# Row pitch of the chunk inputs, in place of a planner that reckons with the arrival of TensorE's instructions

## The chip, the cores and the metric

The kernel runs on one core of one Trainium2 chip. The metric is the device time of one execution in microseconds, lower is better. All data are float32, save the weights, whose inputs can be float64 and are then passed as pairs of 32-bit words.

## The reference

Two layers in a row. The first is a linear attention with a decay for each channel (4 batches, 8 heads, 768 steps, head size 48); the second is a feed-forward layer with a hard-swish gate on the 3072 x 384 result.

```python
for t in range(S):                                   # S = 768
    cur = einsum('bhd,bhe->bhde', u * k[t], v[t])
    y[t] = einsum('bhd,bhde->bhe', r[t], state + cur)
    state = w[t][..., None] * state + einsum('bhd,bhe->bhde', k[t], v[t])
x = y.transpose(0, 2, 1, 3).reshape(3072, 384)       # (batch*step, head*dim)
h = x @ w_in                                         # 384 -> 2048
out = (h * clip(h + 3, 0, 6) / 6) @ w_out            # 2048 -> 384
```

## The kernel before

**Attention.** The 768 steps of each batch are cut into 6 chunks of 128 steps, 24 chunks in all; the two batches of a pair take turns. A chunk's `r`, `k` and `w` come in one row for each channel: the host lays out a tensor `feat` with 112 rows for a chunk (two groups of 48 channels in 64 and 48 partitions), and one row holds 512 numbers of `r`, 512 of `k`, 520 of `w` and one number at the end that makes 1545. `load_feat` moves a chunk's rows in one DMA (chunk 0 in two: `w` first). VectorE then scans the decays backwards (`back_scan`, L509) and forwards (`fore_scan`, L518), which gives scaled copies of the keys (`K`, L529) and queries (`R`, L533, over the scan `W`). TensorE makes scores within half chunks (L584), key transposes (L600), key-value products (L686), the read of the state (L664) and of the values (L673). ScalarE writes the diagonal matrices `A` (L574), VectorE copies the masked scores over them (L591). The state between chunks is decayed and added to on VectorE or GpSimd (L613, L621, L629). For chunks 0 to 8 the product of `r` and `k` is on VectorE (L542) and its sum on TensorE (L556).

**Weights.** Sixteen fetches of 768 KB (`fetch`, L477) bring pairs of weight blocks; ScalarE and VectorE convert them in three steps (`low`, L487; `whole`, L491; `full`, L496, called join below).

**Feed-forward.** Blocks of 4 chunks (512 rows). Block 0 uses plain products (`up`, L802; `down`, L821). Blocks 1 to 5 use a scheme with fewer products and more sums (up products L916, 20 in each half; down products L971, 7 for each pair of chunks), with the clip on ScalarE (L937) and gates and sums on VectorE (L933, L941, L956, L864 to L868).

**Checks of the inputs.** Inputs are loaded once more later on (`refetch`, L1006 and L1011) and reduced on VectorE (`vet`); the result chooses at the end whether a second, general path runs. With these inputs it doesn't.

**What sets the order.** All of these are steps of a `Plan`. Each step has an engine, a duration, the steps that it follows, a key (a due time) and the buffers that it takes and when they come free. `Plan.order` goes through the steps with a clock of its own: at each turn it takes the earliest engine that can start something and, on that engine, the open step with the smallest key. The instructions are emitted in that order, and each engine runs its own in order. So a different plan gives a different order on every engine, and a wait of one instruction holds all behind it on its engine. A table `SHIFT` moves the keys of single steps by hundreds of units.

**Filler.** Until the first up product (`up0.0.0`) the planner fills the time in which it reckons TensorE idle with products of the identity by itself (`spin`, L1357; one unit has 128 columns).

**The model of instruction arrival.** TensorE's instructions come to it by DMA in portions of 256. The planner before counts the instructions of each step (`size`) and reckons in `passed` when a portion is asked for, when it is there, and how late TensorE gets; the lateness is added to the end of the step:

```python
PORTION, ASKED, NEEDED = 256, 168, 194
FETCH, BEHIND, MOST = 3.5, 1.2, 8.0
```

Portion n is asked for when TensorE passes instruction 256n+168, and instruction 256n+194 waits for portion n-1. A portion is reckoned to take 3.5 us, and up to 8 more where the data queue is behind.

Of the kernel before, what the change touches and what calls it, by code (L numbers as in the profile page):

```python
# [19 lines left out]
L = 128  # L20
HL = L // 2
# [28 lines left out]
    "feat0": -505.0, "tok0": -422.0, "own0": 1325.0, "decb0": 271.0, "feat1": -407.0, "tok1": -297.0, "feat2":  # L50
    -455.0, "above2": -94.0, "turn2": 43.0, "read2": 318.0, "R3": 518.0, "least3": 704.0, "diag03": 971.0, "turn3":
    133.0, "read3": 604.0, "fore4": 1319.0, "turn4": 269.0, "fore6": 322.0, "own6": -290.0, "mid6": 481.0, "leave8":
    47.0, "leave9": 373.0, "kvs10": -355.0, "fore11": 329.0, "diag111": 355.0, "turn11": 357.0, "mid11": 685.0,
    "fore13": -285.0, "ownu13": -163.0, "diag013": -196.0, "kvs13": -305.0, "state14": 1259.0, "read14": 59.0,
    "fore15": 1004.0, "sum15": -58.0, "diag015": -247.0, "turn15": 387.0, "kvs15": -268.0, "back16": -161.0,
    "fore16": -243.0, "diag116": 159.0, "kvs16": -365.0, "mid16": -259.0, "read16": -541.0, "diag017": -338.0,
    "kvs17": -427.0, "read17": -508.0, "feat19": 180.0, "tok19": 46.0, "fore19": 666.0, "ownu19": -1100.0, "kvs19":
    -296.0, "leave19": 261.0, "turn20": -251.0, "kvs20": -479.0, "fore21": 290.0, "mid21": -1348.0, "own22": -210.0,
    "tok23": 226.0, "diag023": -1053.0, "turn23": 79.0, "kvs23": -274.0, "read23": -1360.0, "fetch0": -479.0,
    "fetch1": -261.0, "fetch2": -344.0, "fetch3": 259.0, "fetch4": -306.0, "fetch5": 303.0, "low5": -212.0,  # L60
    "fetch7": -138.0, "low7": 805.0, "whole7": -112.0, "full8": -69.0, "whole9": -126.0, "fetch10": 473.0,
    "fetch11": 394.0, "fetch12": 564.0, "fetch13": 285.0, "whole13": 354.0, "fetch14": 586.0, "fetch15": 779.0,
    "up0.3.0": 258.0, "up0.4.0": 306.0, "up0.5.0": 556.0, "up0.9.0": 52.0, "gate0.9.0": -39.0, "up0.13.0": 38.0,
    "gate0.13.0": -156.0, "up0.15.0": 108.0, "up0.8.2": -810.0, "down0.0.0": 410.0, "down0.1.0": 203.0, "down0.1.7":
    314.0, "down0.2.5": 479.0, "up1.0.6": 89.0, "up1.1.14": 306.0, "up1.1.8": 330.0, "up1.1.4": 383.0, "up1.1.9":
    141.0, "up1.1.7": 368.0, "gate1.1.2": -653.0, "gate1.1.5": -825.0, "down1.0.1.0": 463.0, "down1.0.1.1": 593.0,
    "down1.0.2.1": 90.0, "down1.0.3.1": 629.0, "down1.0.7.0": 81.0, "down1.0.4.1": 475.0, "sum1.1.1.1": -773.0,
    "sum1.1.3.1": 659.0, "sum1.1.4.1": 709.0, "down1.1.1.0": 542.0, "down1.1.5.0": 497.0, "down1.1.2.1": 537.0,
    "down1.1.3.0": 301.0, "tx2.6": -780.0, "tx2.10": 959.0, "up2.0.4": -364.0, "up2.0.9": -397.0, "up2.0.10":
    -553.0, "up2.0.16": -156.0, "read2.0.a10": -750.0, "read2.0.a11": -752.0, "read2.0.a15": -340.0, "read2.0.a16":  # L70
    -779.0, "read2.0.a18": -139.0, "gate2.0.1": -90.0, "gate2.0.4": -74.0, "gate2.0.5": 1035.0, "gate2.0.6": -626.0,
    "gate2.0.7": -858.0, "up2.1.14": -190.0, "up2.1.19": -131.0, "up2.1.0": -194.0, "up2.1.8": 293.0, "up2.1.3":
    -188.0, "up2.1.9": -305.0, "down2.0.1.0": -195.0, "down2.0.5.0": 323.0, "down2.0.2.1": 435.0, "down2.0.6.0":
    -341.0, "down2.0.6.1": -14.0, "down2.0.3.0": -16.0, "down2.0.3.1": -340.0, "down2.0.7.0": -347.0, "sum2.1.4.0":
    371.0, "sum2.1.4.1": 756.0, "down2.1.1.1": -157.0, "down2.1.5.0": 394.0, "tx3.7": 1006.0, "up3.0.12": 380.0,
    "up3.0.17": -356.0, "up3.0.11": -442.0, "up3.0.2": 174.0, "up3.0.10": -387.0, "clip3.0.0": 331.0, "gate3.0.1":
    476.0, "up3.1.14": -542.0, "up3.1.6": 187.0, "up3.1.0": -432.0, "up3.1.8": 323.0, "up3.1.4": -456.0, "up3.1.3":
    -451.0, "up3.1.10": -410.0, "up3.1.7": -690.0, "up3.1.16": -464.0, "read3.1.a7": -685.0, "clip3.1.0": -442.0,
    "clip3.1.1": 373.0, "gate3.1.3": 117.0, "sum3.0.1.0": 233.0, "sum3.0.3.0": 438.0, "sum3.0.4.1": 477.0,
    "down3.0.1.0": -218.0, "down3.0.1.1": -245.0, "down3.0.5.0": -244.0, "down3.0.5.1": -247.0, "down3.0.2.0":  # L80
    -324.0, "sum3.1.2.1": -202.0, "down3.1.2.0": 225.0, "down3.1.2.1": -530.0, "tx4.4": 262.0, "up4.0.0": -49.0,
    "up4.0.8": -357.0, "up4.0.17": -342.0, "up4.0.3": -481.0, "read4.0.a10": -634.0, "read4.0.a11": 137.0,
    "read4.0.a16": 85.0, "gate4.0.1": 325.0, "gate4.0.2": 460.0, "gate4.0.3": -218.0, "gate4.0.6": 317.0,
    "up4.1.14": -19.0, "up4.1.19": -324.0, "up4.1.8": 110.0, "up4.1.12": 86.0, "up4.1.13": 35.0, "down4.1.5.1":
    -856.0, "down4.1.2.0": -136.0, "down4.1.2.1": -854.0, "down4.1.6.0": -57.0, "down4.1.6.1": -220.0,
    "down4.1.3.0": -212.0, "down4.1.4.0": -163.0, "down4.1.4.1": -539.0, "out4.1.c12": -607.0, "up5.1.8": 172.0,
    "up5.1.17": 197.0, "up5.1.13": 74.0, "down5.0.3.0": 734.0, "down5.1.1.0": 170.0, "refetch5": 893.0, "refetch8":
    -256.0, "vet8.1": 757.0, "vet10.1": 741.0, "refetch11": -426.0, "refetch12": 327.0, "refetch13": 220.7,
    "vet13.0": 964.0, "vet13.1": 374.0, "vet14.0": -298.0, "vet14.1": -220.0, "refetch15": -25.0, "refetch19":
    145.0, "refetch20": 266.0, "vet20.1": 166.0, "refetch21": 234.0  # L90
# [73 lines left out]
class Plan:  # L164
# [15 lines left out]

    PORTION, ASKED, NEEDED = 256, 168, 194
    FETCH, BEHIND, MOST = 3.5, 1.2, 8.0
    before = 8

    def passed(self, f, t, us, size, link):

        late, i0 = 0.0, f["at"]
        while size > 0 and self.PORTION * f["n"] + self.ASKED < i0 + size:
            asked, needed = self.PORTION * f["n"] + self.ASKED, self.PORTION * f["n"] + self.NEEDED
            asked = max(t + late + us * max(0.0, asked - i0) / size, f["ready"])  # L190
            needed = t + late + us * min(1.0, max(0.0, needed - i0) / size)
            late += max(0.0, f["ready"] - needed)
            f["ready"] = asked + self.FETCH + min(self.MOST, self.BEHIND * max(0.0, link - asked))
            f["n"] += 1
        f["at"] = i0 + max(size, 0)
        return late

    def fills(self, start, last):

        return max(0, int((start - last + self.MORE) / self.SPIN))  # L200

# [9 lines left out]
    def __init__(self):  # L211
        self.steps = {}
        self.size = {}
        self.rings = {}
        self.taken = {}
# [4 lines left out]
    def add(self, name, engine, us, emit, after=(), key=0.0, hold=(), port=False, kb=0.0, lands=0.0,  # L220
            dmas=1, size=0):

        assert name not in self.steps, name
        self.steps[name] = (engine, us, emit, tuple(after), key + SHIFT.get(name, 0.0), tuple(hold), port, kb, lands, dmas)
        self.size[name] = size
# [7 lines left out]
    def order(self):  # L233
# [6 lines left out]
        fetch = {"at": self.before, "n": 0, "ready": 0.0}  # L240
        last, filling = self.COLD, True
# [8 lines left out]
        while open_:  # L250
# [30 lines left out]
            late = 0.0  # L281
            if engine == "PE":
                k = self.fills(t, last) if filling and n != self.until else 0
                filling = filling and n != self.until
                if k:
                    late = self.passed(fetch, t - k * 0.213, k * 0.213, 4 * -(-k // 4), link)
                late += self.passed(fetch, t + late, us, self.size[n], link)
                last = t + us + late
            free[engine] = end[n] = t + us + late
# [25 lines left out]
    def emit(self):  # L315

        last = self.COLD
        spinning = self.spin is not None
        for n in self.order():
            engine, us, emit = self.steps[n][:3]  # L320
            if engine == "PE" and spinning:
                k = self.fills(self.start[n], last) if n != self.until else 0
                while k > 0:
                    self.spin(min(k, 4))
                    k -= 4
                last = self.end[n]
                spinning = n != self.until
            emit()


def fast_path(tc, feat, tok, wflat, ub, ug, moe_w_in, moe_w_out, out, flag, n_chunks):
# [21 lines left out]
    with ExitStack() as ctx:  # L353
# [73 lines left out]

        def load_feat(i):
            a = io.tile([PR, nf], F32, name="feat_in")
# [1270 lines left out]
```

## Time and profile before

| What | Value |
|---|---|
| Time, median of 3 runs | 546.72 us (546.18 to 549.88) |
| Profiled execution, its own time | 546.18 us |
| Its span, first to last instruction | 544.5 us |
| TensorE busy (filler included) | 530.7 us, 97% |
| VectorE busy | 421.7 us, 77% |
| ScalarE busy | 256.1 us, 47% |
| Granted TensorE clock | 0.996 |
| DMA moved | 64.0 MB, 118 GB/s on average |
| Loads of `feat` | 23 of 675.9 KB, one in two parts of 227.9 and 448.0 KB |
| TensorE instruction portions (queue 8) | 44 of 16 KB |

How to read it: the span is 1.7 us shorter than the execution's own time. Busy time is the union of an engine's instructions; a TensorE product's record lasts longer than the distance to the next, so short pauses between two products hide in it. A name like `bank<-xT,w_in` gives what an instruction writes and reads.

### The profile page before, as it was taken

The numbers are of one execution on the slowest core, as the hardware profiler recorded it, in microseconds if no ns is written. First come the engines' busy times: TensorE is split into PE (matmuls) and PEld (weight loads), VectorE is DVE, ScalarE is ACT, GpSimd is POOL, SyncE is SP. The second block draws the span as 40 slices with busy tenths as digits, with TensorE's granted clock in tenths as the row PEclk, the third lists the DMA queues.
The fourth block names the chain that finished last, engine by engine and source line by source line (L and its number), as shares of the span: only waits on it lengthen the run. The fifth ranks groups of instructions, "written<-read, shape, count | busy, mean of one in ns | idle before, by whom it ended". The sixth has DMA issues, their size and how long they took to land.

```text
span 544.5 us, 13050 instructions
## 1 busy us (share of the span) xinstructions
PE 530.7 (97%) x5404; PEld 462.7 (85%) x5404; DVE 421.7 (77%) x701; ACT 256.1 (47%) x656; POOL 112.8 (21%) x111
## 2 busy tenths in 40 slices
PE   8899999999999999999999999999999999999995
PEld 5678877766888999888999977899988999888995
DVE  7999999987479977899668899996998752486440
ACT  4678655443457507464336554644355333363200
POOL 2000002476006123342045123253310000000000
PEclk9999999999999999999999999999999999999998
DMA  8999731645002384466025682074520000000001
GB/s 240 307 296 310 232 130 33 181 131 161 33 1 88 112 239 119 159 197 161 1 79 178 208 238 82 24 208 135 166 111 1 1 23 25 30 0 1 0 16 49
DMA packets 23267, 64.03 MB, mean 118 GB/s; under 512 B 3216, under 2 KB 10544, under 8 KB 23200
## 3 DMA queue, kind: packets, MB, share of 16 engines
q1 hardware_dynamic: 23072, 63.12, 38.5%
q8 instruction: 44, 0.72, 0.6%
q14 instruction: 23, 0.19, 0.1%
q10 hardware_dynamic: 128, 0.00, 0.0%
HBM read 57.31 MB, written 4.72 MB: 114 GB/s over the span
## 4 chain that ended last, share of the span: by engine, by line
PE 85%; DVE 9%; DMA 2%; ACT 1%; issue 1%; POOL 0%; POOLq 0%; DVEq 0%; ACTq 0%
PE bank L971 27%; PE bank L916 24%; PE bank L821 8%; PE bank L802 7%; PE bankS L971 4%; PE bankS L916 4%; DVE g L933 3%; PE bank L686 2%; PE bank L584 2%; PE y_ps L673 2%; PE y_ps L664 2%; DMA bits<-in_moe_w_in_dram 2%; DVE g L941 1%; PE ps L600 1%; PE bankS L1357 1%; PE ps L556 1%
## 5 line engine op out<-in xcount | busy, mean ns | idle before, releaser
L937 ACT ACTIVATE clip<-g,three 128x512 f32<-128x512 f32 x80 | 57.4, 722 | 50.1 <-DVE g L933 38.5
L933 DVE TENSOR_TENSOR g<-bank,g 128x512 f32<-128x512 f32 x80 | 54.1, 685 | 22.7 <-PE bank L916 19.9
L941 DVE SCALAR_TENSOR_TENSOR g<-clip,g 128x512 f32<-128x512 f32 x80 | 56.7, 719 | 7.7 <-ACT clip L937 7.4
L971 PE MATMUL bank<-w_out,g 128*128 128x192 f32 x320 | 57.5, 328 | 0.1
L574 ACT ACTIVATE A<-eyes,dg 128x64 f32<-128x64 f32 x192 | 49.5, 336 | 11.9 <-PE y_ps L673 11.5
L971 PEld LDWEIGHTS bank<-w_out,g 128*128 128x128 f32 x320 | 52.6, 190 | 1.5 <-DVE g L956 0.3
L529 POOL TENSOR_TENSOR K<-feat_in,E 112x512 f32<-112x512 f32 x17 | 21.3, 1252 | 156.1 <-PE bank L584 154.9
L802 PE MATMUL bank<-xT,w_in 128*128 128x256 f32 x192 | 43.8, 381 | 1.1 <-ACT xT L753 0.8
L821 PE MATMUL bank<-w_out,g 128*128 128x384 f32 x128 | 44.1, 491 | 0.0
L769 ACT COPY xT<-y_ps 48x256 f32<-48x256 f32 x88 | 32.2, 366 | 22.9 <-PE y_ps L664 19.0
L916 PE MATMUL bank<-xT,w_in 128*128 128x256 f32 x160 | 41.3, 381 | 0.4 <-ACT g L931 0.4
L931 ACT COPY g<-bank 128x512 f32<-128x512 f32 x50 | 29.0, 585 | 26.9 <-PE bank L916 26.6
L802 PEld LDWEIGHTS bank<-xT,w_in 128*128 128x128 f32 x192 | 35.7, 190 | 6.6 <-ACT xT L753 0.9
L987 ACT ACTIVATE o<-bank 128x192 f32<-128x192 f32 x30 | 9.9, 330 | 62.7 <-PE bank L971 62.6
L821 PEld LDWEIGHTS bank<-w_out,g 128*128 128x128 f32 x128 | 23.5, 190 | 14.1
L518 DVE TENSOR_TENSOR_SCAN W<-feat_in,start 112x520 f32<-112x520 f32 x24 | 32.7, 1367 | 2.5 <-PE y_ps L664 2.3
L509 DVE TENSOR_TENSOR_SCAN E<-feat_in,back 112x520 f32<-112x520 f32 x24 | 32.1, 1336 | 2.9 <-DMA feat_in<-in_feat_dram 2.8
L916 PEld LDWEIGHTS bank<-xT,w_in 128*128 128x128 f32 x160 | 29.9, 190 | 5.0 <-ACT g L931 1.3
L533 POOL TENSOR_TENSOR W<-feat_in,W 112x512 f32<-112x512 f32 x17 | 26.2, 1543 | 30.6 <-DVE W L518 23.2
L613 POOL TENSOR_TENSOR S<-S,w_min 112x192 f32<-112x192 f32 x15 | 14.9, 996 | 81.5 <-DVE S L621 81.5
L916 PE MATMUL bank<-xT,bits 128*128 128x256 f32 x120 | 31.3, 385 | 0.0
L545 POOL TENSOR_TENSOR rk<-rk_in 128x384 f32<-128x384 f32 x15 | 18.2, 1213 | 52.1 <-DMA rk_in<-in_tok_dram 27.8
(274 smaller groups left out, 1125.1 us busy)
## 6 DMA issues: line engine op xcount, KB each, us to landing
feat_in<-in_feat_dram SPq DMA_DIRECT2D x23, 675.9 KB, 5.6
bits<-in_moe_w_in_dram SPq DMA_DIRECT2D x8, 768.0 KB, 10.8
bits<-in_moe_w_out_dram SPq DMA_DIRECT2D x8, 768.0 KB, 7.4
feat_in<-in_moe_w_in_dram SPq DMA_DIRECT2D x8, 768.0 KB, 4.6
feat_in<-in_moe_w_out_dram SPq DMA_DIRECT2D x8, 768.0 KB, 4.7
rk_in<-in_tok_dram SPq DMA_DIRECT2D x15, 384.0 KB, 6.1
v_in<-in_tok_dram SPq DMA_DIRECT2D x24, 192.0 KB, 3.8
out_dram<-o SPq DMA_DIRECT2D x24, 192.0 KB, 2.1
```

Of the source, the lines that this page charges most:

```text
L509: nc.vector.tensor_tensor_scan(out=E_[:, ::-1], data0=d["w"][:, :0:-1], data1=back.rearrange("q p t -> q (p t)")[:, ::-1], initial=0.0, op ...
L518: nc.vector.tensor_tensor_scan(out=W_, data0=d["w"][:, :-1], data1=starts[i % 2].rearrange("q p t -> q (p t)"), initial=0.0, op0=ALU.mult, ...
L574: nc.scalar.activation(out=d["A"][:, h, :], in_=eyes, func=ACT.Copy, scale=d["dg"][:, h])
L769: nc.scalar.copy(out=blocks[bk]["xT"][g * GP:g * GP + D, :, at:at + HL], in_=st[i]["y_ps"][y_bank(i, a, g)][(g ^ a) * GP:(g ^ a) * GP + D, ...
L802: nc.tensor.matmul(h_ps[:, :(c1 - c0) * L], lhsT=w_in[:, f // 2, j, f % 2, :], rhs=b["xT"][:, j, c0 * L:c1 * L], start=(j == 0), stop=(j = ...
L821: nc.tensor.matmul(b["o", c][:, :DM], lhsT=g_of(0, f, c), rhs=w_out[:, f, :], start=(f == 0), stop=(f == NFC - 1))
L916: nc.tensor.matmul(b["p", d, c][:, z * HB:(z + 1) * HB], lhsT=weight(W_PLACE[r])[:, 2 * z + d, :], rhs=x_at(bk, X_PLACE[r]), start=fresh a ...
L931: nc.scalar.copy(out=out_, in_=src)
L933: nc.vector.tensor_tensor(out=out_, in0=src, in1=out_of(bk, d, other), op=ALU.add if sign > 0 else ALU.subtract)
L937: nc.scalar.activation(out=c, in_=out_of(bk, d, u), func=ACT.Relu, bias=three, scale=1.0)
L941: nc.vector.scalar_tensor_tensor(out=g, in0=blocks[bk]["r", d, u], scalar=6.0, in1=g, op0=ALU.min, op1=ALU.mult)
L971: nc.tensor.matmul(b["d", p, to][:, :h], lhsT=a, rhs=w(), start=(f == 0 and k in (1, 5)), stop=(f == HF - 1 and k in (2, 3, 4)), skip_grou ...
```

## The change

The changed kernel differs in three ways.

1. The host pads each row of `feat` from 1545 to 1664 numbers, which is 6656 bytes or 13 times 512. The loads take 1552 numbers of a row (`used`), where they took all 1545.
2. `Plan` has no model of instruction arrival: `passed`, `fills` and `size` are gone, and TensorE's steps last as long as their given durations.
3. The table `SHIFT` is another one: 202 entries where there were 229. Of 69 steps that have an entry in both, none has the same value.

The other constants of the plan are the same, and so are the steps and their given durations. Since both the planner and its table differ, the order of the instructions differs on every engine. The filler is 42 units of 128 columns instead of 39.

```diff
 SHIFT = {
-    "feat0": -505.0, "tok0": -422.0, "own0": 1325.0, "decb0": 271.0, ...
+    "feat0": -208.0, "tok0": -511.0, "own0": 640.0, "feat1": -504.0, ...
 ...
-    def passed(self, f, t, us, size, link):
-        late, i0 = 0.0, f["at"]
-        while size > 0 and self.PORTION * f["n"] + self.ASKED < i0 + size:
-            asked, needed = self.PORTION * f["n"] + self.ASKED, self.PORTION * f["n"] + self.NEEDED
-            asked = max(t + late + us * max(0.0, asked - i0) / size, f["ready"])
-            needed = t + late + us * min(1.0, max(0.0, needed - i0) / size)
-            late += max(0.0, f["ready"] - needed)
-            f["ready"] = asked + self.FETCH + min(self.MOST, self.BEHIND * max(0.0, link - asked))
-            f["n"] += 1
-        f["at"] = i0 + max(size, 0)
-        return late
 ...
-            late = 0.0
-            if engine == "PE":
-                k = self.fills(t, last) if filling and n != self.until else 0
-                filling = filling and n != self.until
-                if k:
-                    late = self.passed(fetch, t - k * 0.213, k * 0.213, 4 * -(-k // 4), link)
-                late += self.passed(fetch, t + late, us, self.size[n], link)
-                last = t + us + late
-            free[engine] = end[n] = t + us + late
+            free[engine] = end[n] = t + us
 ...
+        used = 2 * n + 2 * P * (HL + 1) + 8
+
         def load_feat(i):
-            a = io.tile([PR, nf], F32, name="feat_in")
+            a = io.tile([PR, used], F32, name="feat_in")
             if i == 0:
-                nc.sync.dma_start(out=a[:, 2 * n:], in_=feat[chunk_of[i], :, 2 * n:])
+                nc.sync.dma_start(out=a[:, 2 * n:], in_=feat[chunk_of[i], :, 2 * n:used])
                 nc.scalar.dma_start(out=u_col, in_=ug)
             else:
-                nc.sync.dma_start(out=a, in_=feat[chunk_of[i]])
+                nc.sync.dma_start(out=a, in_=feat[chunk_of[i], :, :used])
 ...
-    end = _np.zeros((NT, GP + D, 1), w.dtype)
+    end = _np.zeros((NT, GP + D, 128 - (2 * P * L + 2 * P * (HL + 1)) % 128), w.dtype)
```

The first instructions of TensorE in the two programs, up to the third up step (turn: key transpose; dot: sum of `r` times `k`; kv: key-value products; read0 and read1: the reads of chunks 0 and 1 in two parts):

```
before: filler 18, turn0, filler 1, score0, dot0, filler 4, kv0, filler 2, dot1, filler 2, turn1, filler 5, score1,
        read0 part 1, filler 3, kv1, read0 part 2, read1 part 1, dot2, filler 4, read1 part 2, dot3, score2,
        six up steps, ...
after:  filler 18, turn0, filler 1, score0, dot0, filler 4, kv0, filler 2, dot1, filler 2, turn1, filler 4, score1,
        read0 part 1, filler 5, kv1, read0 part 2, turn2, filler 3, read1 part 1, filler 1, dot2, kv2, filler 2,
        read1 part 2, score2, dot3, one up step, read of chunk 2, four up steps, ...
```

## The prediction

> **What bounds the kernel now.** I read the page first, then the waits of TensorE, the table of busy time by stretches, the start instruction by instruction, and the DMA records.
>
> ```profile
> span 544.5 us, 13050 instructions
> ...
> PE 530.7 (97%) x5404; PEld 462.7 (85%) x5404; DVE 421.7 (77%) x701; ACT 256.1 (47%) x656; POOL 112.8 (21%) x111
> ...
> q8 instruction: 44, 0.72, 0.6%
> ```
>
> TensorE is busy 530.7 of 544.5 us: 13.8 us are idle in all. Who it waited for (line, releaser, total, times, longest):
>
> ```profile
> PE bankS L1357 <- POOL ident masks.py:199: 1.4, 1, 1.4
> PE bank L743 <- ACT xT L733: 0.9, 1, 0.9
> PE ps L556 <- DVE rk L542: 0.8, 1, 0.8
> PE bank L802 <- ACT xT L753: 0.8, 1, 0.8
> PE bank L971 <- DVE S__3772 L956: 0.6, 1, 0.6
> PE bank L916 <- DVE g L933: 0.6, 1, 0.6
> ```
>
> After 1.4 us ahead of the first instruction, the named waits sum to 5.0 us (these and 0.4, 0.3, 0.2, 0.2, 0.2). The last product ends near 538.4, which leaves a tail of 6.1; 1.3 are crumbs. So the kernel is a nearly unbroken TensorE stream. The exception is its beginning, where TensorE is partly busy with filler products (L1357, ident by ident) until the first up product:
>
> ```profile
> 9.16 1.24 DVE L509 TENSOR_TENSOR_SCAN E<-feat_in,back 112x520 f32<-112x520 f32 x1 [0.83 <-DMA feat_in<-in_feat_dram]
> ...
> 20.95 1.09 ACT L487 ACTIVATE more<-bits 128x768 int16<-128x768 uint8 x1 [1.34 <-DMA bits<-in_moe_w_in_dram]
> ...
> 26.57 1.07 ACT L487 ACTIVATE more<-bits 128x768 int16<-128x768 uint8 x1 [1.78 <-DMA bits<-in_moe_w_in_dram]
> ...
> 29.45 5.45 PE L802 MATMUL bank<-xT,w_in 128*128 128x256 f32 x24 [0.77 <-ACT xT L753]
> ```
>
> and, in the table by stretches (length, then busy PE, PEld, DVE, ACT, POOL, clock, DMA share, GB/s):
>
> ```profile
> 0.00:35.20 35.20, 30.54 (x370) 21.69 (x370) 30.10 (x54) 21.37 (x67) 4.04 (x15) 1.00 0.97 273
> 35.20:60.00 24.80, 24.50 (x328) 20.59 (x329) 24.61 (x49) 20.63 (x57) 0.00 (x0) 1.00 0.88 290
> ```
>
> The reader is to see that up to 60 us VectorE (24.61 of 24.80) and the DMA engines (0.97, 0.88) are full as well: a gain of TensorE alone is given back there.
>
> **The change has three parts, not one:** rows begin at multiples of 512 bytes; the planner loses its model of instruction arrival; and its table of shifts is another one, so the order differs on every engine (I follow it in the listing of the changed program's instructions, engine by engine).
>
> *Rows.* The trace's packets of one feat row (6180 bytes) have a median of 0.356 us and a mean of 0.371; a quarter take 0.236. Rows of 6144 bytes of the refetches, which begin at multiples of 512, have a median of 0.234. A load has 112 rows on 16 engines, 7 each: 7 x (0.371 - 0.236) = 0.9 us less for each of 23 whole loads. This lies behind other work except where somebody waits for it: VectorE waited 2.8 us for feat_in in all, of which 1.06 is the very first load, whose short packets (median 0.086, against 0.088 for aligned 2048 bytes) hardly change. So 0 to 1.7 us there, plus what three loads ahead of the bits take off the 1.34 and 1.78 us that ScalarE waited. Of the VectorE chain I take 0.75 us: the wait of 0.83 at 9.16 goes nearly whole, since rk ends at 8.33 and becomes the bound.
>
> The Trainium skill, "DMA: Bandwidth & Descriptors", section "How a descriptor splits into AXI transactions", says that an unaligned start costs only the unused bytes back to a 256-byte boundary. An estimate by that page is at most 8 beats more on some 193, or 4%, and the gain at the start would be under 0.1 us. The trace's 0.356 against 0.234 speaks for far more, and I go by the trace.
>
> *Planner.* It issues no instruction itself. By its constants, portion n of 256 instructions is asked for at instruction 256n+168 and must be there 282 instructions later. The records of queue 8 (16 KB each) give each landing: in this run it came 1.0 to 8.9 us after that instruction was issued (over 4.9 only in portions 0 to 2, with 6.5, 6.5 and 7.1, and in 31 and 34, with 5.7 and 8.9), while the 282 instructions took at least 4.97 us (portion 28, whose landing took 2.2). The smallest spare time was 2.3 us: no portion was late before. For the new order I summed the products between these points by their rows (a 128x256 product 0.216 us apart, 128x192 0.162, 128x384 0.322, the 64-column ones 0.02); for the old order the same sum gives 5.1 at portion 28, against the 4.97 measured. The tightest new windows are 5.3 (portion 37, about 436 us), 6.0 (30), 6.4 (1 and 8) and 6.5 (26); the landings of those portions before were 1.4, 3.2, 6.5, 1.2 and 2.2. So the new order is no tighter than the old, and only portion 1 may come 0.1 us late, if TensorE waits for nothing else there (it did before: 10.6 us, where the sum says 6.7). Bounds: 0, and 3.7 + 2.9 = 6.6 us if portions 37 and 30 both meet a queue like the longest. I take 0.2, next to the lower end, which the row of portion 1 supports. "Runtime: NRT & Kernel Launch", section "Instruction fetch mechanics", in the Trainium skill calls the crossing of a 16 KiB boundary mostly hidden; by that the term would be 0.
>
> *Order at the start.* The filler grows from 39 to 42 units of 128 columns; 5 units took 1.26 us at 13.40, so +0.7. One key transpose (0.39, start to start of its neighbours) and one group of key-value products (0.61) move ahead of the first up product: they only change place. On VectorE, between the masking of chunk 1 and its decay (L613), there stood rk, more, the back scan and its reciprocal, 0.69+0.60+1.24+0.20 = 2.7; now there stand the scan, reciprocal, more, a decay, a join, K, rk, more: 1.24+0.20+0.60+0.35+0.95+0.67+0.69+0.60 = 5.3. So that decay ends about 21.0 instead of 18.9. Before, chunk 1's read still stood until 23.45, because ScalarE had a `more` waiting for bits ahead of it; now the read comes to 23.0. Its copy-out on ScalarE no longer has a waiting `more` ahead of it: 26.0 instead of 28.45. Then a dot product waits for rk of chunk 3 (about 26.8 on VectorE), takes 1.1, and the first up product follows at about 28.0, not 29.45. With the 1.0 us of work moved ahead TensorE would be 2.5 ahead, filler included.
>
> But VectorE, full until 60, is not: by 28.2 it has then done one `more` (0.6) less, and one state add (0.3) more, than the old order by the same time; it is some 0.3 behind even with 0.75 won by the rows. TensorE's lead therefore turns into waits for joins and gates before 60. I take 0 for the start with rows and filler together; bounds -2.5 (the lead is kept) and +5.3 (the second rival). If the cover of VectorE were gone, the lead itself would be the gain.
>
> *Order behind the start.* The products are the same in number and shape, so only the waits can differ: about 2.3 us of named waits after 60 us. They could go (-2.3) or double (+2.3); I take 0.
>
> **Sum.** Own time of the profiled run 546.2 (span 544.5 and 1.7 around it), start 0, instructions +0.2, rest 0: 546.4. The median of the runs shown stands 0.5 above the profiled run, so the forecast is 546.9 us: no change that shows. A measurement of this kernel can tell about 1% from no change (5.5 us; its three runs spread over 3.7).
>
> **Rivals.** (1) *The start is gained.* Faster rows take the wait out of VectorE and TensorE's lead of 2.5 holds: 546.9 - 2.5 - 0.2 = 544.2. For it: three feat loads stand in the queue ahead of the bits that ScalarE waited for. Against: VectorE at 99%. Past 1% it can hardly go: all named waits (5.0) and crumbs (1.3) gone, with 0.7 of filler more, is 546.7 (the median) - 5.6 = 541.1, just about the bound.
> (2) *TensorE waits for VectorE in the first 60 us; this one ends slower.* The new stream puts chunk 2's read behind one up step only (before, behind many, at 47 us), so TensorE stands until the masking of chunk 2, about 29.4 by the walk above; every slip of VectorE or ScalarE there is paid in full. One slip is a wait for bits like the 1.78 above; three such are 5.3, giving 552.2. It passes 1% from the third slip on. For it: the full engines. Against: earlier landings make those waits shorter.
> (3) *Instructions come late.* Portions 37 and 30 meet a queue like portion 34's: 3.7 + 2.9, less the 0.2 counted, gives 553.3. It starts from a landing over 5.3 us. Against: the DMA engines are nearly idle around 436 us, and the portions of the same places landed within 3.2.
> (4) *The rows don't do what they say*, since the first load was fast anyway and the rest hidden: +0.75, 547.6, inside the forecast.
>
> **How the numbers follow.** Forecast with (4): 0.66. Rival (1): 0.12, of which 0.05 beyond 1%. Rival (2): 0.18, of which 0.16 beyond. Rival (3): 0.04, all beyond; of the forecast's own spread 0.03 lies beyond on the slow side, for waits behind the start. That gives faster 0.05, slower 0.23, same 0.72. The forecast's own range is 545 to 550; to leave out no more than 2 in 10 it reaches down past rival (1) and up past rivals (2) and (3): 543.2 to 553.5.
>
> **What would show it.** Packets of feat rows near 0.24 us; the second scan E at about 8.4 instead of 9.16; the first up product near 28; VectorE still 99% busy to 60, with new waits of TensorE for w_in or gates there; no TensorE gap ending at a landing of queue 8. A first up product after 30, or a gap of over 2 us near portions 1, 30 or 37, would make the forecast wrong to the slow side; TensorE unbroken from 28 on, to the fast side.

## The result and the profile after

The changed kernel takes 546.3 us (median of 20 runs, 543.4 to 548.4). The kernel before, run beside it on the same chip, takes 548.2 (20 runs, 545.8 to 552.4). The ratio is 0.9951, with a 95% interval of 0.993 to 0.9972. So the change gains about half a per cent, where the forecast was no change. Two repeats in other jobs gave 0.9942 (0.9916 to 0.9967) and 0.996 (0.994 to 0.9979).

The profiled execution of the changed kernel takes 547.2 us. Its page, to be set against the lines shown of before, with the granted clock in 40 slices added:

```profile
span 545.5 us, 13085 instructions
...
PE 533.2 (98%) x5408; PEld 466.2 (85%) x5408; DVE 422.4 (77%) x701; ACT 255.1 (47%) x656; POOL 115.6 (21%) x111
...
PEclk9979999999999999999999999999999999999998
```

TensorE is "busy" for 2.5 us more than before, with four products more. But the third slice (27 to 41 us) has a clock of 0.7: products that run slowly count as busy too. Before's profiled execution has no such stretch: at 546.2 us it was one of the quickest of that kernel, while that of the changed kernel is an ordinary one, so the two spans must not be set against each other. The waits of TensorE (line, releaser, total, times, longest):

```profile
PE bank L546 <- ACT w_min L498: 2.5, 1, 2.5
PE bankS L1317 <- POOL ident masks.py:199: 1.4, 1, 1.4
PE bank L648 <- DMA v_in<-in_tok_dram: 0.9, 2, 0.7
PE bank L878 <- DVE T__4259 L830: 0.7, 1, 0.7
PE ps L518 <- DVE rk L504: 0.4, 1, 0.4
PE y_ps L635 <- ACT xT L731: 0.2, 1, 0.2
```

Two things are to be seen. Behind 60 us only the 0.7 and the 0.2 are left; before it was 2.2 (0.6, 0.6, 0.4, 0.2, 0.2, 0.2). And the start has one long new wait, of 2.5 us, ahead of the scores of chunk 2 (L546, which was L584), beside 0.9 us for `v_in`. By stretches:

```profile
0.00:35.20 35.20, 29.59 (x387) 20.57 (x388) 26.08 (x50) 18.19 (x57) 3.01 (x15) 0.93 0.95 248
35.20:60.00 24.80, 24.53 (x324) 20.49 (x324) 21.78 (x41) 18.98 (x52) 0.00 (x0) 0.96 0.74 223
```

Up to 60 us VectorE was busy for 47.9 us, where it was 54.7 before, ScalarE for 37.2 (42.0), and the clock stood at 0.93 and 0.96 where it was 1.00. The start got worse, while the whole got quicker.

**A measure used below.** The *loss* at a time t is t less the time that all products begun until then need at their usual distance (a 128x256 product 0.216 us, 128x192 0.162, 128x384 0.322, and so on; filler counts nothing, and all products together need 518.8 us). I summed it from the trace's list of products. Where TensorE flows, the loss stands still; each stop, filler or slow product raises it. From 60 us to the last product it goes from 17.2 to 19.3 before, and from 22.6 to 21.1 after. (It can sink a little, since the usual distances hold small pauses.) So one half of the answer stands in the two traces already: behind the start the new order loses 3.6 us less, and ahead of it it loses more.

### The profile page after: what moved, and what is told of

It reads as the page before. It is cut to its first block, busy times and chain, and to the rows that moved or that the text cites. A ratio compares the mean times of both kernels' runs of the same rounds, so it can differ in the third digit from the quotient of the medians.

```text
span 545.5 us, 13085 instructions
## 1 busy us (share of the span) xinstructions
PE 533.2 (98%) x5408; PEld 466.2 (85%) x5408; DVE 422.4 (77%) x701; ACT 255.1 (47%) x656; POOL 115.6 (21%) x111
## 4 chain that ended last, share of the span: by engine, by line
PE 93%; DMA 4%; SPq 1%; DVE 1%; issue 1%; ACT 0%; DVEq 0%
PE bank L933 28%; PE bank L878 27%; PE bank L764 8%; PE bank L783 8%; PE bankS L933 5%; PE bankS L878 5%; DMA v_in<-in_tok_dram 4%; PE bank L648 2%; PE bank L546 2%; PE y_ps L635 2%; PE y_ps L626 2%; PE ps L562 2%; PE ps L518 1%; DVE E L471 0%; SPq L439 0%
## 5 line engine op out<-in xcount | busy, mean ns | idle before, releaser
L491 POOL TENSOR_TENSOR K<-feat_in,E 112x512 f32<-112x512 f32 x17 | 24.3, 1428 | 162.1 <-PE bank L546 135.4
L783 PE MATMUL bank<-w_out,g 128*128 128x384 f32 x128 | 42.8, 489 | 0.0
L507 POOL TENSOR_TENSOR rk<-rk_in 128x384 f32<-128x384 f32 x15 | 19.4, 1292 | 94.2 <-PE ps L518 71.9
L893 ACT COPY g<-bank 128x512 f32<-128x512 f32 x50 | 28.5, 586 | 21.1 <-PE bank L878 21.0
L480 DVE TENSOR_TENSOR_SCAN W<-feat_in,start 112x520 f32<-112x520 f32 x24 | 33.9, 1414 | 0.5 <-PE y_ps L626 0.5
L471 DVE TENSOR_TENSOR_SCAN E<-feat_in,back 112x520 f32<-112x520 f32 x24 | 30.4, 1267 | 4.7 <-DMA feat_in<-in_feat_dram 2.4
L495 POOL TENSOR_TENSOR W<-feat_in,W 112x512 f32<-112x512 f32 x17 | 24.5, 1441 | 22.4 <-DVE W L480 22.4
L933 PE MATMUL bankS<-w_out,g 128*128 128x192 f32 x160 | 28.6, 329 | 0.0
```

Source lines behind the costliest of these rows:

```text
L471: nc.vector.tensor_tensor_scan(out=E_[:, ::-1], data0=d["w"][:, :0:-1], data1=back.rearrange("q p t -> q (p t)")[:, ::-1], initial=0.0, op ...
L480: nc.vector.tensor_tensor_scan(out=W_, data0=d["w"][:, :-1], data1=starts[i % 2].rearrange("q p t -> q (p t)"), initial=0.0, op0=ALU.mult, ...
L783: nc.tensor.matmul(b["o", c][:, :DM], lhsT=g_of(0, f, c), rhs=w_out[:, f, :], start=(f == 0), stop=(f == NFC - 1))
L893: nc.scalar.copy(out=out_, in_=src)
L933: nc.tensor.matmul(b["d", p, to][:, :h], lhsT=a, rhs=w(), start=(f == 0 and k in (1, 5)), stop=(f == HF - 1 and k in (2, 3, 4)), skip_grou ...
```

## The experiments

Fifteen kernels ran. Each ratio is to the kernel before, run in the same job.

### The rows alone

Theory: padding shortens the feat loads, and the gain is theirs. Rival: the rows are worth nothing. First the changed kernel without padding, then the kernel before with it:

```diff
-        used = 2 * n + 2 * P * (HL + 1) + 8
+        used = nf
...
-    end = _np.zeros((NT, GP + D, 128 - (2 * P * L + 2 * P * (HL + 1)) % 128), w.dtype)
+    end = _np.zeros((NT, GP + D, 1), w.dtype)
```

> The changed kernel with rows of 1545 numbers again, order and planner of the changed kernel. Theory O (the gain comes from the order behind the first 60 us): as fast as the changed kernel, 0.993 to 0.998 of before; packets of feat rows as in both traces, median 0.33 to 0.36 us. Theory R (the rows bring the gain): the gain is gone, 1.000, and the first loads land later, by some 0.9 us for each.

> The kernel before with rows that begin at multiples of 512 bytes; order, planner and table as before. Theory O: 1.000 of before, within 0.3%. Theory R: 0.995, with the whole gain of the change, and feat packets near 0.24 us.

Measured: 547.9 us, ratio 0.998 (0.9957 to 1.0004), and 548.4 us, 1.0009 (0.9981 to 1.0037). Padding does nothing for the old order. For the new one the first of the two leaves up to 0.4% open; a pair in the last part of this section takes that up. The packets say why: in the old order rows of 6180 bytes had a median of 0.356 us and a mean of 0.371, the padded ones of 6208 bytes 0.353 and 0.371; in the new order it was 0.345 and 0.365 without padding, 0.334 and 0.367 with it.

### Start and rest exchanged

The planner's result is replaced by a fixed list, cut at 60 us of the planner's own time; rows are padded in both. One kernel has before's start and the new rest, the other the reverse.

```diff
-        (Plan.order chooses the next step by its clock)
+        todo = list(GIVEN)    # steps planned to start before 60 us in the one order,
+                              # then all others in the other order
```

> The order of the kernel before for all steps that its planner starts before 60 us, then the order of the changed kernel for the rest; rows as changed; given as a fixed list with the old filler. Theory O: the rest is what wins: TensorE loses some 3.6 us less from 60 us to the end than in the profile before (there +2.2 beyond its own products, in the changed one -1.4), so 0.993 of before or a little less. Theory S (the gain comes from the new start, and the profile of the changed kernel shows a bad case of it): no gain, 1.000.

> The reverse: the changed order for all steps that its planner starts before 60 us, then the order of the kernel before; rows as changed. Theory O: the gain is lost and the start costs something, 1.000 to 1.008. Theory S: 0.995, the gain of the change.

Measured: 548.2 us, ratio 0.9986 (0.9964 to 1.0008), and 565.0 us, 1.0306 (1.0266 to 1.0346). Neither tells the halves apart, since the two lists don't fit at the cut. In the first the loss rises by 2.65 us between 60 and 70 us, and behind that not at all (23.1 at 70 us, 22.9 at the last product). In the second TensorE stands at the cut:

```profile
PE bank L849 <- DVE w_out L524: 8.4, 1, 8.4
PE bank L830 <- DVE g L841: 3.1, 2, 2.1
PE bank L612 <- ACT w_min L564: 2.0, 1, 2.0
```

The 8.4 and 3.1 are weights and gates that the new start has not prepared in the way the old rest wants them. The 2.0 is the new start's own wait again, with the old rest behind it.

### Filler and the clock

The profiles show the granted clock fall to one half for 6.8 us near the start, in all three of the changed kernel, though not in that of before. Of the timed runs only the mean clock is on record; a run with such a drop has a lower one, and I split at 0.9955. By that most runs of both kernels have it. Before: 25 of 29 runs in one job below it, median 549.1, and four above, 546.2. Theory C: TensorE idles too long near 25 to 30 us and the clock drops, so filler put there avoids it. For the changed kernel 10 units go ahead of the scores of chunk 2, for the kernel before 4 each ahead of the read of chunk 1, the dot product of chunk 3 and the first up product. A third kernel has 24 units ahead of before's first up product, to delay TensorE by 5 us and see whether the rest then flows (rival Q: before loses behind 60 us because TensorE is too early there).

```diff
+EXTRA = {"score2": 10}    # in the other two {"read1": 4, "dot3": 4, "up0.0.0": 4}, {"up0.0.0": 24}
...
+                k += EXTRA.get(n, 0)
```

> The changed kernel with 10 more units of filler (2.2 us) between the read of chunk 1 and the scores of chunk 2, where its profile shows TensorE idle for 2.5 us and the granted clock at 0.5 from 30.5 to 37.3 us. Theory C (part of what differs from run to run, and between the two kernels, is whether the clock drops after a stretch in which TensorE stood): the clock stays at 1.0 up to the tail, mean clock 0.999 in most runs, and the median comes to the level of the undisturbed runs of the changed kernel, some 543.5 us or 0.990 of before. Rival (the drop has another cause): mean clock 0.991 to 0.994 in most runs as in the changed kernel, and the time of the changed kernel or up to 2 us more.

> The kernel before with 4 more units of filler at each of three places where its profile shows TensorE idle (ahead of the read of chunk 1, of the dot product of chunk 3, of the first up product). Theory C: the drop goes here too, 546.5 us or 0.995 of before (the level of its three undisturbed runs). Together with the run above this leaves the order behind the start: theory O says that it then stays 2 to 3.6 us slower than the changed kernel with filler. Rival (the change won by dropping the clock less often, and nothing else): both filled kernels take the same time.

> The kernel before with 24 more units of filler (5.2 us) right ahead of the first up product, so that TensorE starts later and the other engines are further ahead. From 60 us to the end TensorE lost 2.2 us beyond its products in the profile before, and won 1.4 in that of the changed kernel. Theory O (it is the order): this stretch still loses about 2 us, and the time is 5 us over that of before without its clock drop, about 551. Rival Q (it is the late start, which gives the other engines slack): the stretch loses 1.5 or less, below nothing perhaps, and the time rises by 2 us at most.

> The changed kernel once more, beside the others on one chip. 0.993 to 0.997 of before. A third of its runs at a mean clock of 0.996 or more and about 544 us, the others at 0.991 to 0.994 and about 547. Set against the run with old rows (0.998): if rows matter it stays clearly below that, if not it comes to 0.997 or 0.998 as well.

Measured: changed kernel with filler 549.2 us, 0.9998 (0.9973 to 1.0024); before with filler 548.3, 0.9981 (0.9951 to 1.0011); before delayed 553.8, 1.0074 (1.0036 to 1.0111); changed kernel again 546.2, 0.9942 (0.9916 to 0.9967).

Theory C holds for the kernel before: with filler 9 of 12 runs are above 0.9955 in mean clock (2 of 31 without). Their median is 547.5, where the two unfilled runs above that mark take 545.8 and 545.9: the filler costs some 1.6 us of the 3 that it saves. Rival Q falls: delayed, the old order still loses 2.8 us behind 60 us. For the changed kernel C fails, and the reason was the clue to the rest. In the list of its TensorE instructions (start, length, ..., idle before and releaser) the filler stands as

```profile
29.78 4.43 PE L1321 MATMUL bankS<-ident 128*128 128x512 f32 x6 [2.68 <-issue]
```

Filler needs nothing but `ident`, loaded long ago, and it waited 2.7 us all the same, for nothing that the profile shows. It stands at the place where the scores of chunk 2 had waited. So it is not what those scores need (`w_min`) that holds TensorE there.

### The late instructions

The records of the instruction queue give the answer. TensorE stands each time behind its product number 345, the last of the read of chunk 1, whatever comes next:

| Kernel | second portion landed | next product begins | behind the landing | gap | put down to |
|---|---|---|---|---|---|
| changed | 30.58 | 32.06 | 1.5 | 2.7 | `w_min` |
| changed, again | 29.16 | 30.79 | 1.6 | 2.8 | `more` |
| changed, third | 30.77 | 32.44 | 1.7 | 3.6 | issue |
| changed, old rows | 29.76 | 31.28 | 1.5 | 3.3 | issue |
| changed, 10 filler | 28.13 | 29.78 | 1.7 | 2.9 | issue |
| new start, old rest | 28.28 | 29.85 | 1.6 | 2.2 | `w_min` |

(Gaps here run from the start of one product to that of the next.) The position fits the model that the change took out: instruction 706, by its constants, is the first that needs portion 1, and product 346 is about there. The portion is asked for at 19 to 21 us, by the same constants; in the six profiles of the table it lands 8 to 10 us later, where before it took 6.5 (it landed at 25.4, and TensorE came to that place only at 28.5). In the new order SP issues `fetch6` (768 KB), the load of chunk 4 (`feat4`, 679 KB) and `tok3` at 21.7, 22.1 and 22.7 us in the profile:

```profile
21.66 0.37 SPq L439 DMA_DIRECT2D bits<-in_moe_w_in_dram  x1
22.09 0.48 SPq L396 DMA_DIRECT2D feat_in<-in_feat_dram  x1
22.66 0.37 SPq L408 DMA_DIRECT2D v_in<-in_tok_dram  x1
```

Before, it issued three fetches, `tok3` and only then, at 24.5, `feat4`:

```profile
19.80 4.12 SPq L477 DMA_DIRECT2D bits<-in_moe_w_in_dram  x3
24.01 0.44 SPq L446 DMA_DIRECT2D v_in<-in_tok_dram  x1
24.50 3.25 SPq L434 DMA_DIRECT2D feat_in<-in_feat_dram  x2
```

By the page, loads and instructions have queues of their own (1 and 8) on the same 16 DMA engines. Theory I: the portion is late beside these transfers. Rival V: VectorE's chain sets the end of the gap. The test moves one DMA in the fixed list of the new order and changes no other engine's order; a second kernel adds 4 units of filler ahead of the scores of chunk 2.

```diff
-  ... fetch6 feat4 ... tok3 ... fetch7 ... feat5 ... fetch1 ... score2 ...
+  ... fetch6 ... tok3 ... fetch7 feat4 ... feat5 ... fetch1 ... score2 ...
```

> The changed kernel with one DMA moved: the load of chunk 4 (feat4, 679 KB) is issued behind fetch7 (and so behind tok3) instead of right behind fetch6; every other engine's order is that of the changed kernel. In the changed kernel's trace, its repeat, the one with old rows and the one with filler, TensorE stands for 2.7, 2.8, 3.3 and 2.9 us behind the same product (number 345, the last of read1) whatever comes next, and goes on 1.5, 1.6, 1.5 and 1.7 us after the second transfer of the instruction queue has landed (30.58, 29.16, 29.76, 28.13). Theory I (portion 1 of TensorE's instructions is late, since feat4 and tok3 stand ahead of it in the data queue): with feat4's 2.5 us out of its way the portion lands 2 to 3 us earlier, at 26 to 27.5, the gap behind product 345 shrinks from 2.7 to under 1.5 us (what remains is the wait for w_min, done at 29.5 in two of the runs), the half clock behind it may go, and the time falls by 1 to 3.5 us: ratio to the kernel before 0.987 to 0.993. Theory V (VectorE's chain up to E of chunk 2 and w_min sets the end of the gap): the gap stays at 2.5 to 3 us, ratio 0.995. Loss at 60 us by I 18.5 to 20.5, by V 21.5 to 22.5.

> As the run before, and 4 units of filler (one product of 512 columns) ahead of score2. Theory I: the instructions are there, so the filler starts within 0.3 us of the end of read1 (in the kernel with 10 units of filler and feat4 in its old place it waited 2.7 us for nothing that the profile shows), no window of 3.4 us falls under 2.4 us of products, the granted clock stays at 1.0 up to 60 us (mean 0.995 or more in most of the runs), and the ratio to the kernel before is 0.986 to 0.992. Theory V, or if the portion is still late: the filler waits over 1.5 us again, the clock halves for 6.8 us as before, ratio 0.996 to 1.0.

Measured: 542.7 us (4 runs), ratio 0.9888 (0.987 to 0.9906), and 544.1 us, 0.9916 (0.9886 to 0.9945). The portion landed at 24.68 and 26.09, the gaps are 0.03 and 0.15 us, and all ten runs have a mean clock of 0.997 or more. That is what theory I foretold (the portion even earlier than its 26 to 27.5), and V did not: the gap is gone with no change to VectorE's order. Then the same kernel again, beside a twin with the old rows:

> The kernel with feat4 issued later once more, unchanged, with padded rows. If the 0.9888 found (4 runs) stands, 0.987 to 0.991, TensorE goes on from read1 to score2 without a gap of over 0.5 us, and the clock stays at 1.0 up to 60 us in most of the runs (mean 0.995 or more). By a chance find instead: 0.993 or more.

> The kernel with feat4 issued later, with the rows of before (1545 numbers, no padding); its padded twin runs in the same job. Theory R (padding is worth 1 to 2 us with this order: the changed kernel measured 0.9951 and 0.9942 of before, and 0.998 with old rows): ratio to before 0.991 to 0.993 against 0.987 to 0.990 of the twin. Theory N (padding is worth nothing: packets of 6208 bytes have a median of 0.334 us against 0.356 of 6180, and with before's order padding gave 1.0009): the same ratio as the twin within 0.002. In both, portion 1 of TensorE's instructions is there in time and TensorE doesn't stand behind product 345.

Measured: 544.3 us, 0.9932 (0.9906 to 0.9958), and with old rows 543.95 us, 0.9923 (0.9895 to 0.995). With the new order too, padding gives nothing that shows; with 6 and 9 runs a microsecond either way can't be ruled out. But 0.9932 is less than 0.9888, and the profile of that run has the old gap once more:

```profile
27.02 0.55 PE L701 MATMUL bank<-A,v_in 64*48 64x64 f32 x24
29.56 1.13 PE L612 MATMUL bank<-W,K 48*64 48x64 f32 x32 [1.99 <-ACT w_min L564]
```

The portion had landed at 27.97 there, 1.6 us ahead of the 29.56. With one load moved, its landing differs from run to run by over 3 us, and here it was late; why it was late in this run is not shown. The last job therefore ran the changed kernel, the one with `feat4` later, and one in which `fetch6` too goes behind `tok3`, side by side:

> The changed kernel once more, beside the next two on the same chip. By all theories 0.994 to 0.996 of before, a gap of 2.5 to 3.3 us behind product 345 that ends 1.5 to 1.7 us after the second landing of the instruction queue, and mean clock under 0.9955 in over half of the runs.

> The changed kernel with feat4 issued behind fetch7, for the third time, beside the changed kernel itself. Theory I (the late portion, and the half clock behind it, cost the changed kernel 2 to 3.5 us, and moving feat4 away avoids it in over half of the runs): 0.989 to 0.993 of before, 2 to 3.5 us under the changed kernel's median of this job, mean clock of 0.9955 or more in over half of the runs. If the first find was chance: within 1 us of the changed kernel.

> As the run before, and fetch6 (768 KB, 2 us of the data queue) is issued behind tok3, so that nothing of the weights stands ahead of portion 1 when it is asked for at about 19.3 us. Theory I: the portion lands at 22 to 25 us in nearly all runs, never late; TensorE goes from read1 to score2 without a gap of over 0.5 us, and nearly all runs are undisturbed: 0.987 to 0.991, unless the weights of fetch6, 1 to 2 us later, make the first up steps wait (then a wait for w_in of 0.5 to 1.5 us shows, and 0.990 to 0.994). Theory V (VectorE's chain): the gap stays.

| Kernel | median, us (12 runs) | ratio, interval | runs with mean clock over 0.9955 |
|---|---|---|---|
| changed | 546.8 | 0.996 (0.994 to 0.9979) | 2 |
| `feat4` later | 544.4 | 0.9929 (0.9902 to 0.9956) | 10 |
| `feat4` and `fetch6` later | 543.8 | 0.9922 (0.9893 to 0.995) | 11 |

Both versions beat both kernels, by 2.4 and 3.0 us against the changed one; between themselves they can't be told apart. The last expectation was missed in part: with `fetch6` moved too, the portion landed at 26.05, not at 22 to 25, and TensorE went on 1.5 us behind it, after a gap of 0.29. Moving `fetch6` too adds nothing that shows, and how the portion finds its turn among the loads stays open. Nor is it shown that all of the 2.4 us is the portion's: the waits for `v_in` of 0.3 to 1.1 us in the changed kernel's three profiles are gone too, now that `feat4` is issued behind `tok3`. A line of TensorE's waits in the changed kernel's third profile, and the list of TensorE's instructions at the same place with `feat4` later, show the difference:

```profile
PE bank L546 <- issue: 3.4, 1, 3.4
```

```profile
26.67 0.55 PE L701 MATMUL bank<-A,v_in 64*48 64x64 f32 x24
27.04 0.65 PE L612 MATMUL bank<-W,K 48*64 48x64 f32 x32
27.62 1.15 PE L584 MATMUL ps<-u_col,rk 112*128 112x112 f32 x8
28.60 1.47 PE L830 MATMUL bank<-xT,w_in 128*128 128x256 f32 x6
```

The first up product (L830) begins at 28.60; in the first profile of the changed kernel it began at 34.96. And the two stretches around the gap, of the changed kernel (length, busy PE, PEld, DVE, ACT, POOL, clock, DMA share, GB/s):

```profile
27.30:30.50 3.20, 2.22 (x47) 1.86 (x46) 2.08 (x4) 3.07 (x13) 0.00 (x0) 1.00 1.00 223
30.50:37.40 6.90, 5.34 (x46) 4.50 (x46) 5.01 (x11) 3.53 (x12) 0.00 (x0) 0.51 1.04 252
```

and with `feat4` later:

```profile
27.30:30.50 3.20, 3.20 (x74) 2.70 (x65) 3.06 (x9) 3.11 (x11) 0.00 (x0) 1.00 1.02 217
30.50:37.40 6.90, 6.20 (x69) 5.03 (x60) 3.61 (x7) 4.85 (x14) 0.00 (x0) 1.00 1.00 241
```

With the gap TensorE is busy for 2.2 of 3.2 us, then gets half the clock for 6.8 us and begins 46 products there instead of 69. One late transfer of 16 KB is paid twice: all seven profiles with this gap have the half clock at that place, and none of the five of the new start without it.

The next portion is not far off either. In three of these five TensorE stops once more, at product 473, 1.5 us behind the landing of that portion (34.45 in this profile), for 0.3 to 0.6 us (here its line among TensorE's waits with `feat4` later):

```profile
PE bank L830 <- issue: 0.6, 1, 0.6
```

Whether the old planner, with its model of arrival, would have avoided these stops was not tried.

## Why the prediction was wrong, step by step

The forecast was no change, and the kernel became 0.5% faster. The step that failed is the order behind the start, put at 0 for want of a reason to choose a sign: there the new order loses 3.6 us less. A second step failed the other way: the instructions, put at +0.2, cost a gap of 2.7 to 3.6 us in the changed kernel's profiles and brought the half clock, which hid part of the gain. That 546.9 stands so near the measured 546.3 is luck: the base was too low, and the two errors have opposite signs.

**Base.** The sum began at the profiled run's 546.2 and added 0.5 for the median. That run had no half clock, as only a few runs of before have (9 of 89 over three jobs; they run at 546 where the others take 549). The usual time of before is 548 to 549, so the same kernel unchanged would have been forecast 2 us too low. The three times shown, 546.2 to 549.9, span both kinds (only the first has its clock on record), and I read them as spread.

**Instructions: +0.2, at portion 1.** The place was right, and the size was wrong. I bounded the landing of each portion by the landing of the same portion before (6.5 us for portion 1), and compared only the new order of TensorE with it. The new order of SP issues other loads about when the portion is asked for; it took 8 to 10 us, and the gap was 2.2 to 3.6 us. My own condition stood in the text ("may come 0.1 us late, if TensorE waits for nothing else there"): a margin of nothing, priced as if the landing were fixed. Rival (3) had the mechanism, but at portions 30 and 37, and those came in time (smallest spare time 1.2 us; the one stop near portion 37 is about 0.2 us, wherever the landing falls).

**Order at the start: 0.** The walk through the engines gave the first up product near 28.0, if nothing else were late. With the portion in time and no filler added it is 28.5 to 29.1 in four profiles (29.45 before), so the walk was nearly right. It was also right that TensorE's lead would not last: the loss with `feat4` later is 1.7 us below before's at 30 us, 0.9 at 40 and 0.1 at 60. In the changed kernel as it is, the up products begin at 33.7 to 35.3. "A first up product after 30 ... would make the forecast wrong to the slow side": it came after 30, and the kernel was still quicker, since I had counted nothing in the other direction.

The scan expected at 8.4 us was another reading of one run as if it were the kernel's. It begins at 8.3 to 10.8 in twelve profiles of the new start, at 10.77 in that of the changed kernel, its wait is put down mostly to the landing of chunk 1's load, and it doesn't go with the rows (10.55 and 9.01 with the old ones; 9.2 to 10.3 in five profiles of the old start).

```profile
10.77 1.24 DVE L471 TENSOR_TENSOR_SCAN E<-feat_in,back 112x520 f32<-112x520 f32 x1 [2.26 <-ACT dg L526]
```

The releaser `dg` in this line of VectorE's list is not something that the scan reads; in the repeat, 2.35 us at the same place are put down to `feat_in`.

**Order behind the start: 0, between -2.3 and +2.3.** The step that decided the sign, and the largest error. From 60 us to the last product the loss rises by 2.1 to 2.8 us with before's order (four profiles: as it is, with padding, with filler, delayed), and sinks by 0.4 to 1.5 with the new one (eleven profiles). A part is named in the waits: 1.6 us on sums and gates between 318 and 346 us, where before's loss rises by 2.1 us, are not in the changed kernel (the 0.6 and 0.6 shown in the prediction, and this one):

```profile
PE bank L916 <- ACT g L931: 0.4, 1, 0.4
```

In all, the named waits behind 60 us go from 2.2 to 0.9; the rest of the 3.6 us no wait names. So the difference lies beyond the lower bound of -2.3 (all named waits go). To take the middle, since a new order could as well be worse, was a guess, and the list of the new order held what might have decided it: how early each gate and sum stands ahead of the product that needs it. I did not follow it behind 60 us.

**Rows: 0.9 us a load.** A quick quarter of the packets (0.236; it is nearer a fifth) was taken as the price of an aligned row. Alignment is not what made them quick: with all rows aligned, the mean is 0.371 in the old order, as before, and 0.367 in the new. I weighed here a rule of the Trainium skill ("DMA: Bandwidth & Descriptors", section "How a descriptor splits into AXI transactions") against my row, and it was nearer the measurement: by it I had estimated 4% at most, and the mean differs by 1% or less.

**The books.** Set beside each other at full clock, before runs at 546.2 us (4 of 29 runs of the last job) and the new order without the late portion at 543.9 (10 of 12): 2.3 us. The loss at 60 us is the same in their profiles (17.2 and 17.1), which puts the 2.3 us behind the start; but each is one profile, and in one with the portion in time and old rows (a run of 546.0 us) that loss was 3 us higher, so for the timed runs the split is argued and not shown. In the usual runs, with the late portion in the one and the half clock in both, 2.2 us stay (546.8 against 548.9). How much of the 2.7 us and of the half clock behind it is paid again by other waits was not measured apart. Also open is which change of the table makes the rest flow: both exchanges of halves failed at the cut.

## What to carry to other kernels

When the order of a program changes, the order of its loads changes with it, and everything that shares the DMA engines with them, the instructions of an engine included, can have a new landing time; a bound taken from the old landing holds only if what moves beside it is the same. Where one engine stops at the same instruction under changing names of releasers, ask what else that instruction needs: filler put at the place, which needs nothing, tells an operand from an instruction that isn't there. And compare the clock of the profiled run with that of the timed runs before using its span as the base of a sum.

## What the runs showed of the hardware

TensorE goes on 1.5 to 1.7 us after the portion of instructions that it stands for has landed (seven profiles with a gap of over 2 us at portion 1; 1.5 us in three with a shorter one at the next). "Runtime: NRT & Kernel Launch", section "Instruction fetch mechanics", in the Trainium skill calls the crossing from one 16 KB block to the next mostly hidden. That holds for nearly all of the 44 portions here, and not for portion 1 with 1.6 MB of loads issued within 1.2 us about when it was asked for: there the gap was 2.2 to 3.6 us.

The granted clock went to 0.5 near the start in ten of the seventeen profiles, for 6.83 us in nine and 3.41 in one. In the 3.41 us ahead of the drop TensorE was busy for 1.4 to 2.4 us. "TensorE: Matmul & The Clock Gate", section "What's actually happening", puts the drop behind an idle window of about 3.4 us that runs free of the program. The length of the steps agrees (3.41 us, and 6.83 as two of them), but the stretch was not idle. A stretch of 3.41 us with 1.8 us of products passed without a drop in before's profile. That the window runs free would fit this, and that the same program drops in some runs and not in others; no run here shows its phase.
